# Reading the inverse row sums instead of every q and k block in the range check of an unshifted exp

## The chip, the cores and the metric

The kernel runs on one core of a Trainium2 chip. The metric is the device time of one execution in microseconds. A core has five engines that run side by side, each through its own queue: PE (TensorE, matrix products), VectorE (DVE in the profile), ScalarE (ACT), GpSimd (POOL) and SyncE (SP). Medians are quoted with the range of their runs.

## The reference

Two independent attention problems, A and B, whose outputs are put side by side. The shapes are 2048 tokens, width 1024, 32 heads of 32, and a causal window of 256 keys.

```python
def _A_ref(x, wqkv, wo):                       # _B_ref is the same
    B, S, D = x.shape
    H = 32; Dh = D // H; W = 256
    qkv = (x @ wqkv).reshape(B, S, 3, H, Dh)    # q, k, v, heads in front
    scores = einsum("bhqd,bhkd->bhqk", q, k) * (Dh ** -0.5)
    mask = (i - j >= 0) & (i - j < W)
    p = softmax(where(mask, scores, -1e9))
    return (p @ v, heads merged) @ wo
```

x and both weights are 0.05 times normal numbers in bf16.

## The kernel before

The quick path takes exp(score - SHIFT) with a constant SHIFT instead of the row's maximum. That is right only while the scores are moderate, so a check runs beside it, and if it fails, a slow path with a true softmax computes everything again. Before, the check ORs the bits of every q and k block into one tile `top`, and at the end compares the largest magnitude seen with 2.0.

The program is not written in the order of its execution. A planner in Python deals out matmul chains and, for each result in PSUM (one of two banks, `pp`), picks the engine that copies it to SBUF, with a crude clock of its own for each engine. VectorE's smaller work waits in a list `side`.

```python
class _Clock:
    def evacuate(self, engines):
        best = min(engines, key=lambda e: max(getattr(self, e), self.pe) + COST[e])
        end = max(getattr(self, best), self.pe + 150.0) + COST[best]
        setattr(self, best, end)
        ...
def evacuate(out, in_, engines=("act", "dve")):
    if clock.evacuate(engines) == "act":
        nc.scalar.copy(out=out, in_=in_)
    else:
        nc.vector.tensor_copy(out=out, in_=in_)
def add_or(dst):                       # after each evacuated q or k block: the end of the list
    def f():
        nc.vector.tensor_tensor(out=top[:], in0=top[:], in1=dst.bitcast(I32),
                                op=ALU.bitwise_or)
    side.append((COST["or"], f, False))
...                                    # in pv(), per pair of query blocks, after its matmuls into acc
    def f():
        nc.vector.reciprocal(out=rinv[:], in_=acc[:, 2 * P:3 * P])
    pieces.append((COST["rinv"], f, False))
    def f():
        for h in range(2):
            nc.vector.stream_shuffle(out=wide[:, h * P:(h + 1) * P], in_=rinv[:], ...)
        nc.vector.tensor_tensor(out=oTs[...], in0=acc[:, 0:256], in1=wide[:], op=ALU.mult)
    pieces.append((COST["mult"], f, True))
    n = max([i + 1 for i, x in enumerate(side) if x[2]], default=0)
    side[n:n] = pieces                 # ahead of waiting ORs
...                                    # in the main loop: an edge is two additions for a pair's row sums
    while edges_due and edges_due[0][0] <= now:
        edge(*edges_due.pop(0)[1:])
    ...
    if now >= sealed and len(certify) == 2:
        while side:
            run_side()
        certify.pop(0)(top)            # AND, maximum, comparison on VectorE
    elif now >= sealed + 2 and len(certify) == 1:
        certify.pop(0)(ps_proj)        # 1x1 matmul: sum of the verdicts, read by VectorE
```

## Time and profile before

The median was 609.52 us (609.34 to 609.76, 3 runs).

| engine | busy us | share | what it does |
|---|---|---|---|
| PE | 593.6 | 98% | projections, scores, attention, output |
| VectorE | 468.4 | 77% | additions, reciprocals, shuffles, multiplies, ORs, 66 evacuations |
| ScalarE | 441.1 | 73% | 180 exps, 189 evacuations of 512 columns |
| GpSimd | 326.3 | 54% | masks |

An engine at 98% leaves nothing for the others to shorten except its waits. The prediction below shows those lines.

### The profile page before, as it was taken

The page shows a single profiled execution, that of the slowest core. Times are in us where ns is not written, and L with a number is a line of the kernel's source. Part 1 is how long each engine was busy: PE and PEld are TensorE (multiplying, and loading weights), DVE is VectorE, ACT ScalarE, POOL GpSimd, SP SyncE. Part 2 cuts the span into 40 slices and gives each one's busy share as a digit, 9 for nine tenths or more (in the row PEclk, how much of TensorE's full clock was granted, in tenths as well). Part 3 has the DMA queues.
Part 4 walks back from the last instruction along what each step waited for, and adds up shares of the span by engine and source line. Part 5 has one row for each costly group of instructions (what it writes and reads, how often), then busy time and mean ns, then how long its engine had stood idle before and what let it go on. Part 6 is the DMA issues. An engine that isn't in the chain of part 4 may idle for free.

```text
span 607.6 us, 28768 instructions
## 1 busy us (share of the span) xinstructions
PE 593.6 (98%) x12786; PEld 344.3 (57%) x12838; DVE 468.4 (77%) x1199; ACT 441.1 (73%) x376; POOL 326.3 (54%) x630
## 2 busy tenths in 40 slices
PE   8999999999999999999999999999999999999996
PEld 6555466656655756564556756655455665545443
DVE  1677889898898898897888887898888887897200
ACT  3778887788888887877778877777776777785332
POOL 0565666665666666556555565555555655554000
PEclk9999999999999999999999999999999999999999
DMA  9833110111015501442111100112021040113222
GB/s 234 182 92 89 37 38 3 38 38 39 3 38 90 114 14 30 82 101 77 38 37 38 38 4 8 33 37 81 2 68 34 4 106 21 55 58 120 72 79 64
DMA packets 86802, 35.47 MB, mean 58 GB/s; under 512 B 65552, under 2 KB 86160, under 8 KB 86672
## 3 DMA queue, kind: packets, MB, share of 16 engines
q1 hardware_dynamic: 85632, 33.31, 22.2%
q8 instruction: 102, 1.67, 1.2%
q10 hardware_dynamic: 1040, 0.26, 0.2%
q14 instruction: 28, 0.23, 0.1%
HBM read 17.83 MB, written 8.39 MB: 43 GB/s over the span
## 4 chain that ended last, share of the span: by engine, by line
PE 96%; ACT 2%; issue 1%; DMA 1%; ACTq 0%
PE pp L176 44%; PE pp L172 28%; PE acc L513 13%; PE st L451 10%; ACT pt L459 1%; DMA oT<-in_A_x_dram 1%; PE acc L582 0%; PE pp L568 0%; ACT kT L190 0%; ACT vt L190 0%; PE st L582 0%; ACT osb L190 0%; PE pp L805 0%; ACTq L190 0%
## 5 line engine op out<-in xcount | busy, mean ns | idle before, releaser
L459 ACT ACTIVATE pt<-st 128x2048 bf16<-128x2048 f32 x180 | 338.0, 1878 | 91.6 <-PE st L451 73.5
L471 POOL TENSOR_SCALAR_AFFINE_SELECT pt<-pt 128x512 bf16<-128x512 bf16 x224 | 154.5, 690 | 145.7 <-ACT pt L459 143.1
L467 POOL TENSOR_SCALAR_AFFINE_SELECT pt<-pt 128x512 bf16<-128x512 bf16 x256 | 179.2, 701 | 85.8 <-ACT pt L459 85.8
L524 DVE RECIPROCAL rinv<-acc 128x128 f32<-128x128 f32 x128 | 122.0, 953 | 57.0 <-PE acc L513 56.4
L176 PE MATMUL pp<-xT,wqk 128*32 128x512 bf16 x2712 | 163.1, 379 | 0.0
L481 DVE TENSOR_TENSOR both<-pt 128x512 bf16<-128x512 bf16 x224 | 137.1, 651 | 0.0
L176 PEld LDWEIGHTS <-wqk 128*32 128x32 bf16 x2712 | 69.3, 97 | 54.2 <-issue 0.4
L172 PE MATMUL pp<-xT,wqk 128*128 128x512 bf16 (+1 forms) x323 | 76.7, 369 | 4.1 <-issue 2.4
L176 PE MATMUL pp<-wv,xT 128*32 128x256 bf16 x2436 | 75.9, 273 | 0.0
L451 PE MATMUL st<-qT,kT 32*128 32x384 bf16 (+2 forms) x1488 | 71.5, 269 | 0.1
L176 PEld LDWEIGHTS <-xT 128*32 128x32 bf16 x2436 | 63.8, 97 | 6.2
L529 DVE STREAM_SHUFFLE wide<-rinv 128x128 f32<-128x128 f32 x256 | 64.6, 298 | 0.0
L513 PE MATMUL acc<-pt,vt 128*32 128x128 bf16 (+1 forms) x2160 | 63.3, 239 | 0.0
L172 PE MATMUL pp<-wo_sb,oT 128*128 128x512 bf16 (+1 forms) x269 | 59.3, 373 | 1.3 <-issue 0.9
L451 PEld LDWEIGHTS <-kT 32*128 32x128 bf16 x1488 | 22.2, 92 | 64.5 <-issue 63.3
L190 ACT CAST osb<-pp 128x512 bf16<-128x512 f32 (+1 forms) x52 | 30.0, 577 | 39.1 <-PE pp L172 24.4
L531 DVE TENSOR_TENSOR oT<-acc,wide 128x256 bf16<-128x256 f32 x128 | 54.3, 425 | 4.4
L176 PE MATMUL pp<-wo_sb,oT 128*32 128x512 bf16 x952 | 55.6, 379 | 0.0
L172 PEld LDWEIGHTS <-wqk 128*128 128x128 bf16 x362 | 33.4, 98 | 37.0 <-issue 6.8
L172 PE MATMUL pp<-wv,xT 128*128 128x256 bf16 x415 | 50.9, 273 | 1.4 <-ACT kT L190 0.6
L513 PEld LDWEIGHTS <-vt 128*32 128x32 bf16 x2160 | 35.9, 96 | 26.4 <-issue 24.1
L172 PEld LDWEIGHTS <-xT 128*128 128x128 bf16 x415 | 38.9, 98 | 12.0 <-issue 6.1
(46 smaller groups left out, 386.5 us busy)
## 6 DMA issues: line engine op xcount, KB each, us to landing
out_dram<-osb SPq DMA_DIRECT2D x63, 128.0 KB, 1.8
wqk<-in_B_wqkv_dram SPq DMA_DIRECT2D x32, 128.0 KB, 2.5
wqk<-in_A_wqkv_dram SPq DMA_DIRECT2D x24, 128.0 KB, 2.7
wo_sb<-in_A_wo_dram SPq DMA_DIRECT2D x16, 128.0 KB, 2.2
wv<-in_B_wqkv_dram SPq DMA_DIRECT2D x16, 128.0 KB, 2.8
wo_sb<-in_B_wo_dram SPq DMA_DIRECT2D x16, 128.0 KB, 2.4
oT<-in_A_x_dram SPq DMA_DIRECT2D x4, 256.0 KB, 5.4
wv<-in_A_wqkv_dram SPq DMA_DIRECT2D x2, 512.0 KB, 5.9
```

Of the source, the lines that this page charges most:

```text
L172: nc.tensor.matmul(out[:, lo:hi], lhsT=lhsT, rhs=rhs, start=start, stop=stop, skip_group_check=True)
L176: nc.tensor.matmul(out[c:c + 32, lo:hi], lhsT=lhsT[:, c:c + 32], rhs=rhs, start=start, stop=stop, tile_position=(0, c), skip_group_check=True)
L190: nc.scalar.copy(out=out, in_=in_)
L451: nc.tensor.matmul(st[:, r, a:b, :], lhsT=kT[32 * r:32 * r + 32, j * P:(j + 1) * P], rhs=qT[32 * r:32 * r + 32, q * P:(q + b - a) * P], st ...
L459: nc.scalar.activation(out=pt[:, :, :n, :].rearrange("p r a q -> p r (a q)"), in_=st[:, :, :n, :].rearrange("p r a q -> p r (a q)"), func= ...
L467: nc.gpsimd.affine_select(out=blk, in_=blk, pattern=[[0, 4], [1, P]], compare_op=ALU.is_ge, fill=0.0, base=0, channel_multiplier=-1)
L471: nc.gpsimd.affine_select(out=blk, in_=blk, pattern=[[0, 4], [-1, P]], compare_op=ALU.is_gt, fill=0.0, base=0, channel_multiplier=1)
L481: nc.vector.tensor_tensor(out=both[:, :, h, :], in0=pts[s0][:, :, a0, :], in1=pts[s1][:, :, a1, :], op=ALU.add)
L513: nc.tensor.matmul(acc[32 * r:32 * r + 32, o:o + w_], lhsT=lhsT, rhs=src[:, r, :, :], start=(x == 0), stop=(x == len(moves) - 1), tile_pos ...
L524: nc.vector.reciprocal(out=rinv[:], in_=acc[:, 2 * P:3 * P])
L529: nc.vector.stream_shuffle(out=wide[:, h * P:(h + 1) * P], in_=rinv[:], mask=[16 * h] * 32)
L531: nc.vector.tensor_tensor(out=oTs[(pi, k)][:, t, (p % 2) * 256:(p % 2 + 1) * 256], in0=acc[:, 0:256], in1=wide[:], op=ALU.mult)
```

## The change

The intent is to relieve VectorE. A softmax row whose scores are moderate has a sum, and so an inverse, within a known power-of-two range, and the inverse is there anyway. One operation per two pairs XORs its bits with 2.0's and ORs them into `top`; bits 29 and 30 must stay clear. As the last inverse comes at the end, so does the verdict. SHIFT changes so that the inverses fall into the range.

```diff
+IN_RANGE = 0x40000000
+OUT_OF_RANGE = 0x60000000
+SHIFT = 33.0 * math.log(2.0) - math.log(1.9)
...
                     evacuate(dst, st_["pp"][:])
-                    add_or(dst)
...
-        rinv = normp.tile([P, P], F32, name="rinv")
+        turn = g * NP + p
...
+            if turn % 2 == 0:
+                inverses[0] = normp.tile([P, 2, P], F32, name="rinv")
+            nc.vector.reciprocal(out=inverses[0][:, turn % 2, :], in_=acc[:, 2 * P:3 * P])
...                                   # in the multiply's piece, behind the multiply
+            if turn % 2:
+                nc.vector.scalar_tensor_tensor(
+                    out=top[:], in0=inverses[0][:].rearrange("p h q -> p (h q)").bitcast(I32),
+                    scalar=IN_RANGE, in1=top[:], op0=ALU.bitwise_xor, op1=ALU.bitwise_or)
-        pieces.append((COST["mult"], f, True))
+        pieces.append((COST["mult"] + (COST["or"] if turn % 2 else 0.0), f, True))
...                                   # the verdict: out of the loop, behind the last multiply
     finish_norm()
+    certify[0](top)
+    emit(END + 10, 2 * NS_MM * CT)
+    certify[1](ps_proj)
     emit(END + 10, float("inf"))
```

More of the change, by code (lines that the diff above doesn't have):

```diff
@@ L20 @@
 KEYS_PER_QUERY = 3 * P
-CERT = 30.0
-SHIFT = 53.0 * math.log(2.0) - math.log(1.9)
-assert SHIFT >= CERT + math.log(KEYS_PER_QUERY)
+IN_RANGE = 0x40000000
+OUT_OF_RANGE = 0x60000000
+SHIFT = 33.0 * math.log(2.0) - math.log(1.9)
+assert math.log(KEYS_PER_QUERY) < SHIFT < 62.0 * math.log(2.0)
 MASK_NEG = -1.0e9
-QK_LIMIT = 2.0
-QK_LIMIT_BITS = 0x4000
 QB = 4
@@ L122, in _fast_path @@
     edges = {}
+    inverses = [None]
     top = once.tile([P, 256], I32, name="top")
@@ L180, in _fast_path @@
     whole = [True]
-    def add_or(dst):
-        def f():
-            nc.vector.tensor_tensor(out=top[:], in0=top[:], in1=dst.bitcast(I32),
-                                    op=ALU.bitwise_or)
-        side.append((COST["or"], f, False))
     def evacuate(out, in_, engines=("act", "dve")):
@@ L523, in f @@
         def f():
-            nc.vector.reciprocal(out=rinv[:], in_=acc[:, 2 * P:3 * P])
+            if turn % 2 == 0:
+                inverses[0] = normp.tile([P, 2, P], F32, name="rinv")
+            nc.vector.reciprocal(out=inverses[0][:, turn % 2, :], in_=acc[:, 2 * P:3 * P])
         pieces.append((COST["rinv"], f, False))
@@ L528, in f @@
             for h in range(2):
-                nc.vector.stream_shuffle(out=wide[:, h * P:(h + 1) * P], in_=rinv[:],
+                nc.vector.stream_shuffle(out=wide[:, h * P:(h + 1) * P], in_=inverses[0][:, turn % 2, :],
                                          mask=[16 * h] * 32)
@@ L603, in _fast_path @@
     emit(0, chains[0].size)
-    sealed = first_use(G - 1, NQ - 1, 0)
     for now in range(END):
@@ L616, in _fast_path @@
         emit(now, level(now) - fixed[now])
-        if now >= sealed and len(certify) == 2:
-            while side:
-                run_side()
-            certify.pop(0)(top)
-        elif now >= sealed + 2 and len(certify) == 1:
-            certify.pop(0)(ps_proj)
-    assert not certify
     while edges_due:
@@ L793 @@
     consts = {"ones": ones, "ident": ident}
-    assert DH * QK_LIMIT * QK_LIMIT * cfg.scale <= CERT
     def reduce_bits(top):
         seen = top[:]
-        nc.vector.tensor_single_scalar(out=seen, in_=seen, scalar=0x7FFF7FFF, op=ALU.bitwise_and)
-        nc.vector.tensor_reduce(out=pm[:], in_=seen.bitcast(I16), axis=AX.X, op=ALU.max)
-        nc.vector.tensor_scalar(out=okp[:], in0=pm[:], scalar1=float(QK_LIMIT_BITS), scalar2=None,
+        nc.vector.tensor_single_scalar(out=seen, in_=seen, scalar=OUT_OF_RANGE, op=ALU.bitwise_and)
+        nc.vector.tensor_reduce(out=pm[:], in_=seen, axis=AX.X, op=ALU.max)
+        nc.vector.tensor_scalar(out=okp[:], in0=pm[:], scalar1=0.5, scalar2=None,
                                 op0=ALU.is_lt)
```

## The prediction

> **What bounds the kernel now.** I read the page first, for the engine that has no slack. Columns: busy time, share of the span, instructions; then the busy share in 40 slices.
>
> ```profile
> PE 593.6 (98%) x12786; PEld 344.3 (57%) x12838; DVE 468.4 (77%) x1199; ACT 441.1 (73%) x376; POOL 326.3 (54%) x630
> ...
> PE   8999999999999999999999999999999999999996
> ...
> DVE  1677889898898898897888887898888887897200
> ```
>
> PE is at 9 tenths or more in every slice but the first and the last, DVE is not full in any long stretch. A busy PE is not yet a PE that never waits, so the second view is PE's waits between 10 and 565 us, that is without the start and the tail (columns: engine and line, what it waited for, us in total, times, longest).
>
> ```profile
> PE pp L172 <- issue: 3.5, 22, 0.2
> PE pp L172 <- ACT vt L190: 1.0, 2, 0.5
> PE pp L172 <- ACT kT L190: 0.6, 2, 0.4
> PE pp L172 <- DVE oT L531: 0.3, 2, 0.2
> ```
>
> 5.4 us in 555. The "issue" part belongs to PE's own stream, and the two DVE entries are 0.16 us each, as long as the usual issue gap, so I count them with it. What other engines really cost PE in the loop is four stalls of ScalarE, 0.39 + 0.49 + 0.49 + 0.19 = 1.56 us. Third, the chain that ended last, at one of the four, says how they arise:
>
> ```profile
> 71.84 0.36 PE st L451 x8
> 72.20 0.02 issue
> 72.22 1.88 ACT pt L459
> 74.10 0.49 ACT kT L190
> 74.58 0.04 issue
> 74.63 0.38 PE pp L172 x2
> ```
>
> A projection ended just after an exp had started, ScalarE could evacuate its PSUM bank only behind that exp, and the next projection but one needed the bank. VectorE is in none of the four. So VectorE, where the whole change lies, has 1.56 us of PE time within its reach at the very most, and only if it takes such an evacuation over. Fourth, the groups of instructions, for prices (count, busy us, mean ns, idle before them):
>
> ```profile
> L184 DVE TENSOR_TENSOR top<-top,kT 128x256 int32<-128x256 int32 x64 | 35.2, 549 | 0.9 <-ACT kT L190 0.5
> L184 DVE TENSOR_TENSOR top<-top,qT 128x256 int32<-128x256 int32 x64 | 32.4, 507 | 1.9 <-ACT qT L190 1.3
> L192 DVE CAST kT<-pp 128x512 bf16<-128x512 f32 x19 | 12.9, 678 | 7.8 <-PE pp L176 5.1 <-PE pp L172 2.7
> ```
>
> **What the Trainium skill says.** "TensorE: Matmul & The Clock Gate", section "Wait — 56ns, not 53.3ns?", gives a warm matmul a pitch of N / 2.4 GHz + about 2.5 ns, 215.7 ns at 512 columns. In the tail the evacuations of eight-matmul chains start 1.727 us apart, 215.9 ns per matmul: PE streams at its rate there, and a saving elsewhere cannot speed it up. "VectorE: DVE Perf Modes", section on the TRN2 errata, gives an fp32 tensor_tensor of N elements (N + 151) / 0.96 ns, 424 ns at 256; the ORs' medians are 417 ns (q) and 464 ns (k), so it holds for undisturbed ones. Their means of 507 and 549 fit "SBUF — State Buffer", section "Who interferes with whom": a DVE instruction with two SBUF inputs contends with a GpSimd one that reads SBUF, and the later one blocks. The trace has ORs from 407 up to 896 ns and GpSimd selects from 628 up to 924 ns. The new operation also has two SBUF inputs, so I price it as the old one. "DVE: scalar operands, raw-bit mode, write accounting and state across instructions", section 2, says that an immediate in bit-vector mode is a raw 32-bit pattern; the old check ends with such an AND and its run took the fast path, so I expect the new XOR and AND to be exact too.
>
> **The change part by part.**
> 1. Removed: 128 ORs over q and k blocks, 35.2 + 32.4 = 67.6 us of VectorE.
> 2. Added: one XOR-then-OR per two pairs, 128 / 2 = 64, over 128x256 words. At the ORs' mean, (549 + 507) / 2 = 528 ns, that is 33.8 us (estimate). It stands right behind the multiply that frees the accumulator, so it does not delay that release.
> 3. Moved by the planner: it counts VectorE as less loaded and gives it more evacuations. In the built order I count 79 PSUM evacuations of 512 columns on VectorE, before 66; 176 on ScalarE, before 189. At 674 ns (the mean of the 66) VectorE gets 13 x 0.674 = 8.8 us more, at 584 ns ScalarE gets 7.6 us less. Sum: VectorE 468.4 - 67.6 + 33.8 + 8.8 = 443 us (73%), ScalarE 441.1 - 7.6 = 433.5 us (71%). All of it lies beside PE's stream.
> 4. PE: its instruction order is identical in both, GpSimd's too, but for one instruction, the 1x1 matmul that adds up the verdict. So PE's work is the same to the instruction, and its time changes only by waits.
> 5. The waits in the loop. I went through the order for every reuse of a projection bank that ScalarE evacuates and compared when PE wants the bank with when the evacuation can end (exp 1.88 us, evacuation 0.59 us, matmuls at the pitch above). In the kernel before, the four tightest places are the four stalls of the trace, with 0.55 to 0.86 us too little; those that lack 0.35 us or less did not stall. The stall is thus about the lack less 0.35 us. In the changed order the four are gone, VectorE evacuates there, but five others lack 0.85, 0.75, 0.66, 0.55 and 0.45: 0.50 + 0.40 + 0.31 + 0.20 + 0.10 = 1.5 us. Net 0.0.
> 6. The verdict. Before, it is decided inside the loop:
>
> ```profile
> 556.99 0.16 PE L805 MATMUL pp<-okp,ones 128*1 128x1 f32 x1
> ...
> 557.01 0.16 PE L805 MATMUL pp<-okp,ones 128*1 128x1 f32 x1
> 557.04 0.49 PE L513 MATMUL acc<-pt,vt 128*32 128x128 bf16 x17
> ...
> 557.22 0.14 DVE L806 TENSOR_SCALAR unsafe_i<-pp 1x1 int32<-1x1 f32 x1 [1.15 <-PE pp L805]
> ...
> 557.57 3.64 PE L176 MATMUL pp<-wo_sb,oT 128*32 128x512 bf16 x64
> ```
>
> The next projection writes the same bank and waits until VectorE has read the sum, but 0.9 us of attention matmuls go in between, so it costs PE nothing. In the changed order the sum stands between two output projections of the tail, and the very next matmul waits for VectorE's read (the bank is the same, the order shows the wait). From 556.99 to 557.36 plus some 0.05 us of signalling: PE stands still for about 0.4 us. That lies on the path: +0.4 us.
> 7. Is the sum's own input late? The last multiply ends at 567.8; the XOR (0.9 at most), AND, reduction and comparison (0.61 + 0.69 + 0.15 in the old check) end by 570.2. PE gets to the sum after 32 matmuls from 565.71, at 572.6. No wait. After it come 16 whole and two half stores, near 29 us, so the branch at the end finds its verdict ready.
>
> Sum: 609.5 + 0.0 + 0.4 = 609.9 us.
>
> **The rivals.** (a) VectorE's relief speeds the kernel: 77% busy and 25 us less to do looks like a gain. For it: an engine that lags would free banks and accumulators late. Against it: no PE wait on VectorE beyond the issue gap. It can give back 1.56 us at most if all four stalls go and no new one comes: 608.4 with the tail's cost. (b) More VectorE evacuations stall PE instead: its queue is in order, and an evacuation behind a reciprocal (0.95 us), shuffles and the 0.65 us additions comes late. For it: 13 more of them, and the new operation keeps the reciprocal's successor waiting. Against it: 66 such evacuations caused no stall. Five stalls of 0.4 us would make 611.9. (c) The check fails and the slow path runs: many times the time. The scores here are close to 0 (x and w are 0.05 times normal numbers), so a row sum of 1 to 256 keys is about 1.9 x 2^-33 times that count, its inverse 2^24 to 2^32; bit 30 is set and bit 29 clear from 2 to 2^65. I give it under 1%. (d) The check at the end lengthens the finish, because the sum waits for VectorE or all engines for the verdict: part 7 leaves 2.4 us and 29 us of slack.
>
> **Range and chances.** Runs of the kernel before span 0.4 us. Part 5 is the uncertain one, from -1.5 to +1.5 us; new VectorE stalls lean upwards. Predicted 609.9, range 608.7 to 611.2. Two per cent is 12 us, more than all waits of PE in the loop together (5.4), so faster by that is all but excluded (0.01); slower needs the slow path or a failure of the order (0.02); the same 0.97.
>
> **What would show it.** VectorE near 443 us and ScalarE near 433 us busy; 64 new operations at 0.42 to 0.6 us; PE busy 593 to 594 us; in PE's waits four to six ScalarE evacuations of 1 to 2 us in total, at other times than before; one wait of about 0.4 us on VectorE's read of the verdict near 573 us. I am wrong if VectorE evacuations appear in PE's waits with over 1 us, if PE's busy time moves by more than 1 us, or if the ScalarE stalls vanish altogether.

## The result, and the profile after

The changed kernel took 611.24 us (611.07 to 611.60, 4 runs) beside 609.64 us of before: ratio 1.0027, interval 1.0010 to 1.0045. It is slower by 1.6 us, where +0.4 was predicted; 611.24 lies just outside the range that ended at 611.2.

The first line of the page after (busy us, share, instructions):

```profile
PE 599.8 (98%) x12838; PEld 345.0 (57%) x12838; DVE 437.3 (72%) x1148; ACT 434.8 (71%) x363; POOL 317.8 (52%) x630
```

VectorE lost 31 us and ScalarE 6, as intended. PE's busy time seems to have grown by 6 us, but it has 12838 matmul records here, as many as weight loads, and only 12786 before: the trace before lacks 52. The gaps that they leave had been listed there as 22 "issue" waits, 3.5 us in all. After, there are none. All thirteen traces agree: the eight with 12786 records list an "issue" wait, the five with 12838 list none. PE's waits after (what it waited for, us in total, times, longest; the first is the start):

```profile
PE pp L567 <- DVE ones L777: 1.3, 1, 1.3
PE pp L172 <- ACT qT L184: 0.8, 3, 0.4
PE acc L506 <- DVE oT L526: 0.7, 1, 0.7
PE pp L172 <- ACT vt L184: 0.5, 1, 0.5
PE pp L172 <- ACT kT L184: 0.4, 1, 0.4
PE pp L172 <- DVE unsafe_i L799: 0.2, 1, 0.2
```

There are five ScalarE stalls (0.8 + 0.5 + 0.4 = 1.7 us), the wait for the verdict, and one that the prediction did not have: PE waits 0.70 us for an accumulator that VectorE's multiply (oT) frees late.

Both traces hold the same weight loads in the same order, so subtracting their start times shows where the time is lost. Each number is a step of the difference "after minus before"; the offset of 0.15 us at the start is left out, since it varies between -0.3 and +0.9 us from profile to profile.

```
us        step    what PE's waits show there
75        -0.35   ScalarE stall of before gone
126       +0.57   new ScalarE stall (0.41 idle)
142       -0.65   stall of before gone
147       +0.78   late accumulator (0.70 idle)
158, 174  +0.25, +0.35   new ScalarE stalls (0.19 idle each)
225, 242  -0.50, -0.66   stalls of before gone
374, 385  +0.55, +0.63   new ScalarE stalls (0.39, 0.50 idle)
572       +0.49   verdict (0.24 idle)
rest      +0.38   (100: +0.17, 117: +0.09, 251: +0.16, 319: -0.17, 487: +0.13)
sum       +1.84
```

The sum agrees with the 1.6 us of the timed runs to their scatter. Gone are 2.16 us, new at ScalarE 2.35, VectorE's late accumulator 0.78, the verdict 0.49 (the weight loads of the verdict's own sum are left out when the traces are aligned; 0.3 of it is the wait for VectorE, the rest the small sum itself).

A stall costs up to 0.17 us more than its idle time. This is how the profile counts: the record of a 512-column matmul lasts 379 ns, but the next one starts after 216 ns, so idle time begins only 163 ns after the next matmul could have started. The starts say the same: 788 ns apart at 126 us, and 788 - 216 = 572 ns is the step there.

How the accumulator comes late is in the chain that ended last, which here leaves PE and runs along VectorE (start us, us, engine and tile):

```profile
140.29 0.95 DVE rinv L519
141.24 1.18 DVE both L474 x2
142.41 0.54 DVE vt L186
142.95 0.50 DVE wide L524 x2
...
143.81 0.69 DVE top L529
144.50 1.54 DVE both L474 x2
146.04 0.88 DVE rinv L519
...
147.97 0.74 PE acc L506 x36
```

The planner had given the v block at 142.4 us to VectorE. Its queue is in order. Two additions and this evacuation (1.18 and 0.54 us) stood between a reciprocal (done at 141.2) and that reciprocal's shuffles and multiply, so these ran at 142.95 to 143.9. VectorE was not idle before the evacuation, so it lost no time there by waiting for its matmul. Then the new operation (0.69 us) and two more additions stood in front of the next reciprocal, and the next multiply ended at 147.9 instead of 147.0. Before, shuffles and multiply followed the reciprocal at once and were done at 141.6, and the next reciprocal had 1.02 us to spare (VectorE's timeline of the kernel before, idle time in brackets):

```profile
139.66 0.95 DVE L524 RECIPROCAL rinv<-acc 128x128 f32<-128x128 f32 x1
140.65 0.29 DVE L529 STREAM_SHUFFLE wide<-rinv 128x128 f32<-128x128 f32 x1
...
141.19 0.42 DVE L531 TENSOR_TENSOR oT<-acc,wide 128x256 bf16<-128x256 f32 x1
141.53 0.41 DVE L184 TENSOR_TENSOR top<-top,kT 128x256 int32<-128x256 int32 x1
141.86 0.75 DVE L481 TENSOR_TENSOR both<-pt 128x512 bf16<-128x512 bf16 x2
142.53 0.42 DVE L184 TENSOR_TENSOR top<-top,qT 128x256 int32<-128x256 int32 x1
142.87 1.19 DVE L481 TENSOR_TENSOR both<-pt 128x512 bf16<-128x512 bf16 x2
145.07 0.96 DVE L524 RECIPROCAL rinv<-acc 128x128 f32<-128x128 f32 x1 [1.02 <-PE acc L513]
...
146.62 0.42 DVE L531 TENSOR_TENSOR oT<-acc,wide 128x256 bf16<-128x256 f32 x1
```

The verdict in the tail (timeline: start us, us, engine, line, operation, tiles, idle before it):

```profile
574.18 0.19 PE L798 MATMUL pp<-okp,ones 128*1 128x1 f32 x2
...
574.41 0.15 DVE L799 TENSOR_SCALAR unsafe_i<-pp 1x1 int32<-1x1 f32 x1 [3.86 <-PE pp L798]
574.61 5.55 PE L172 MATMUL pp<-wo_sb,oT 128*128 128x512 bf16 x25 [0.24 <-DVE unsafe_i L799]
```

PE goes on 0.43 us after it began the sum, as the prediction had it. VectorE had idled 3.86 us, so the sum did not wait for the check.

The groups of the new operation and of the additions after (count, busy us, mean ns, idle before):

```profile
L474 DVE TENSOR_TENSOR both<-pt 128x512 bf16<-128x512 bf16 x224 | 126.5, 605 | 0.8 <-PE acc L506 0.8
...
L529 DVE SCALAR_TENSOR_TENSOR top<-rinv,top 128x256 int32<-128x256 int32 x64 | 37.0, 578 | 0.0
```

### The profile page after: what moved, and what is told of

The parts are those of the page before. It is cut to its first block, busy times and chain, and to the rows that moved or that the text cites. A ratio compares the mean times of both kernels' runs of the same rounds, so it can differ in the third digit from the quotient of the medians.

```text
span 609.6 us, 28777 instructions
## 1 busy us (share of the span) xinstructions
PE 599.8 (98%) x12838; PEld 345.0 (57%) x12838; DVE 437.3 (72%) x1148; ACT 434.8 (71%) x363; POOL 317.8 (52%) x630
## 4 chain that ended last, share of the span: by engine, by line
PE 73%; DVE 3%; issue 1%; ACT 1%; DVEq 0%; ACTq 0%
PE pp L176 34%; PE pp L172 22%; PE acc L506 11%; PE st L444 7%; DVE both L474 1%; DVE rinv L519 1%; DVE wide L524 1%; ACT pt L452 0%; DVE top L529 0%; DVE oT L526 0%; DVE vt L186 0%; ACT qT L184 0%; ACT kT L184 0%; ACT vt L184 0%; ACT osb L184 0%
## 5 line engine op out<-in xcount | busy, mean ns | idle before, releaser
L464 POOL TENSOR_SCALAR_AFFINE_SELECT pt<-pt 128x512 bf16<-128x512 bf16 x224 | 149.4, 667 | 153.1 <-ACT pt L452 153.1
L460 POOL TENSOR_SCALAR_AFFINE_SELECT pt<-pt 128x512 bf16<-128x512 bf16 x256 | 175.6, 687 | 88.2 <-ACT pt L452 88.2
L474 DVE TENSOR_TENSOR both<-pt 128x512 bf16<-128x512 bf16 x224 | 126.5, 605 | 0.8 <-PE acc L506 0.8
L172 PE MATMUL pp<-xT,wqk 128*128 128x512 bf16 (+1 forms) x362 | 82.7, 370 | 0.6 <-ACT qT L184 0.6
L172 PE MATMUL pp<-wo_sb,oT 128*128 128x512 bf16 (+1 forms) x282 | 61.4, 373 | 0.2 <-DVE unsafe_i L799 0.2
```

The source lines that it names most:

```text
L172: nc.tensor.matmul(out[:, lo:hi], lhsT=lhsT, rhs=rhs, start=start, stop=stop, skip_group_check=True)
L460: nc.gpsimd.affine_select(out=blk, in_=blk, pattern=[[0, 4], [1, P]], compare_op=ALU.is_ge, fill=0.0, base=0, channel_multiplier=-1)
L464: nc.gpsimd.affine_select(out=blk, in_=blk, pattern=[[0, 4], [-1, P]], compare_op=ALU.is_gt, fill=0.0, base=0, channel_multiplier=1)
L474: nc.vector.tensor_tensor(out=both[:, :, h, :], in0=pts[s0][:, :, a0, :], in1=pts[s1][:, :, a1, :], op=ALU.add)
```

## The experiments

My first theory after the result: the evacuations moved by the planner cost 0.3 us net at ScalarE, the new operation makes the accumulator at 148 us late (0.8), the verdict costs 0.4. Its rivals: the operation as such costs everything; the moved evacuations cost everything. All eleven kernels gave right results and had five timed rounds; those of one heading ran on one chip with the same runs of before.

### First group (before: 609.50 us, 609.05 to 609.97)

**b_no_or**: before, ORs not issued. The check then guards nothing, on purpose.

```diff
-            nc.vector.tensor_tensor(out=top[:], in0=top[:], in1=dst.bitcast(I32),
-                                    op=ALU.bitwise_or)
+            pass
```

> The kernel before with its 128 ORs not issued; the planner and so every other instruction and its place are unchanged (the check then guards nothing, the result stays right). Theory 1 (PE bounds the kernel, VectorE's load lies beside it): VectorE's busy time falls by 67 us to about 400, the time stays within 0.4 us of 609.6, and the four ScalarE stalls (74, 143, 227, 244 us) stay. Rival (VectorE's load, or its contention with GpSimd for the SBUF port, slows the whole): 608.5 us or less.

Measured 610.03 us (608.87 to 610.09), ratio 1.0001 (0.9987 to 1.0015). VectorE's busy time fell from 468.4 to 400.8 us, the 67.6 us of the ORs to the tenth, and the four ScalarE stalls stayed where they were. The ORs cost nothing that these runs resolve (the interval leaves about 0.8 us either way; the aligned traces end 0.27 us ahead), so there was next to nothing to save by a cheaper check, with the rest in its place.

**a_no_op**: the changed kernel, new operation not issued; the planner still counts it.

```diff
-            if turn % 2:
-                nc.vector.scalar_tensor_tensor(
-                    out=top[:], in0=..., scalar=IN_RANGE, in1=top[:],
-                    op0=ALU.bitwise_xor, op1=ALU.bitwise_or)
```

> The changed kernel with its 64 XOR-OR operations not issued, everything else in its place. Theory 1 (the 1.6 us are: one late accumulator at 148 us for 0.8, five ScalarE stalls against four for 0.3, the verdict for 0.4): the operation at 143.8 us (0.69 us) delays the accumulator, so that the wait of 0.70 us at 148 us goes; the five ScalarE stalls and the verdict's wait stay; 610.4 us. Rival A (the operation itself costs the 1.6 us): 609.6. Rival B (only the moved evacuations cost, the operation nothing): 611.2, the wait at 148 us stays.

Measured 611.15 us (610.91 to 611.32), ratio 1.0026 (1.0012 to 1.0040). My first theory missed: without the operation the time is as good as the same. In the trace an accumulator is still late, at 150.75 us and by 0.44 instead of 0.70 us. By the aligned traces this kernel ends 1.31 us behind before, the changed one 1.83, so the operation may cost up to 0.5 us in this setting; the times do not resolve it.

**a_own_bank**: the changed kernel, the verdict's sum in an accumulator bank.

```diff
-        csum = pool.tile([P, 512], F32, name="pp")
+        csum = pool.tile([P, 512], F32, name="acc")
-    certify[1](ps_proj)
+    certify[1](ps_acc)
```

> The changed kernel with the verdict's sum in an accumulator bank that is free in the tail, so that the next projection need not wait for VectorE's read. Theory 1: the gap of about 0.4 us at 574 us goes, 610.8 us. Rival (the gap is the small matmul itself, or nothing is won since the end waits for the verdict): 611.1 to 611.3.

Measured 610.86 us (610.58 to 611.74), ratio 1.0023 (1.0009 to 1.0036). In the trace the wait is gone: PE goes on at 574.62 after a sum begun at 574.50. The verdict's step in the aligned traces falls from 0.49 to 0.2 us, so a part of it is the small sum itself and stays, as the rival had it; at the end this kernel is 1.45 us behind before, not 1.83. The times agree in sign, but their intervals overlap.

**b_after_plan**: before, each evacuation on the engine that the changed kernel uses. PLAN is the changed kernel's list of 257 choices. (Forced onto its own list, each kernel gave its own program again, instruction by instruction.)

```diff
-        best = min(engines, key=lambda e: max(getattr(self, e), self.pe) + COST[e])
+        best = {"a": "act", "d": "dve"}[PLAN[self.n]]
+        self.n += 1
```

> The kernel before, ORs and early verdict as they were, but each of its 257 evacuations on the engine that the changed kernel uses (43 differ). Theory 1: the five ScalarE stalls of the changed kernel (126, 159, 176, 375, 385 us) appear, the four of before go, +0.3 us; the accumulator at 148 us is late too if the evacuations in front of it suffice, which gives up to +0.8 more: 609.9 to 610.8 us. Rival (the placement costs nothing, only the new operation and the verdict do): 609.6 us.

Measured 611.47 us (611.22 to 612.05), ratio 1.0036 (1.0022 to 1.0049): above the expected range, and as slow as the changed kernel, with the old ORs and the early verdict. PE's waits of this run, without the start:

```profile
PE pp L180 <- DVE vt L200: 1.0, 2, 0.7
PE pp L180 <- ACT qT L198: 0.6, 2, 0.4
PE pp L180 <- ACT vt L198: 0.5, 1, 0.5
PE pp L180 <- ACT kT L198: 0.4, 1, 0.4
PE pp L180 <- DVE kT L200: 0.3, 1, 0.3
```

Four of the changed kernel's five ScalarE stalls are listed here (the fifth is too short for the list, but its step of 0.35 us is in the aligned traces), and where before had ScalarE stalls (143, 227, 245 us) PE now waits for VectorE's evacuations. Moving 43 evacuations, with nothing else changed in the mathematics, makes the slowdown by itself.

### Second group (before: 609.79 us, 609.10 to 610.27)

My second theory: placement costs the loop its time, the operation nothing.

**a_before_plan**: the changed kernel with before's list of 257 choices in PLAN, otherwise the edit of b_after_plan.

> The changed kernel with every one of its 257 evacuations on the engine that the kernel before uses: the new operation and the late verdict alone, without the moved evacuations. Theory 2 (the moved evacuations cost the loop its time, the operation nothing; the verdict 0.3 us): the four ScalarE stalls of before are back (74, 143, 227, 244 us), the five of the changed kernel and the late accumulator at 148 us are gone, the verdict's wait stays: 609.9 us. Rival (the new operation in its place costs as well): 610.6 us or more.

Measured 611.06 us (610.49 to 611.57), ratio 1.0023 (1.0009 to 1.0036). The second theory fell too. The four ScalarE stalls were back and the five and the late accumulator gone, as expected, but two steps of 0.24 and 0.34 us were new at 374 and 384 us. There PE waited for a v block on VectorE (0.20 us idle at 384.69). VectorE in front of it (timeline):

```profile
382.38 0.55 DVE L537 SCALAR_TENSOR_TENSOR top<-rinv,top 128x256 int32<-128x256 int32 x1
382.85 1.18 DVE L482 TENSOR_TENSOR both<-pt 128x512 bf16<-128x512 bf16 x2
383.96 0.68 DVE L194 CAST vt<-pp 128x512 bf16<-128x512 f32 x1
```

The new operation stands ahead of the evacuation. In the kernel before, the ORs came behind the same evacuation, because they were the end of the list:

```profile
381.66 1.32 DVE L481 TENSOR_TENSOR both<-pt 128x512 bf16<-128x512 bf16 x2
382.91 0.68 DVE L192 CAST vt<-pp 128x512 bf16<-128x512 f32 x1
383.51 0.41 DVE L184 TENSOR_TENSOR top<-top,qT 128x256 int32<-128x256 int32 x1
```

**a_side_first**: the changed kernel with its own choices forced, but before VectorE is given an evacuation, all pending work is issued.

```diff
         else:
+            while side:
+                run_side()
             nc.vector.tensor_copy(out=out, in_=in_)
```

> The changed kernel, same engine for each evacuation, but before VectorE is given an evacuation all pending reciprocal and multiply work is issued to it. Theory 2 says that the accumulator at 148 us is late because VectorE's in-order queue held that work behind an evacuation (142.3 us) that still waited for its matmul: the wait of 0.7 us goes, the five ScalarE stalls and the verdict stay, 610.5 us. Rival (the work in front makes the evacuations late in turn): new VectorE waits in PE's list, 611 us or more.

Measured 622.16 us (622.01 to 622.36), ratio 1.0205 (1.0191 to 1.0219): the rival, and far more of it than expected. Two of its wait lines:

```profile
PE pp L180 <- DVE vt L196: 2.1, 3, 1.0
PE pp L180 <- DVE kT L196: 1.9, 6, 0.6
```

The late accumulator did vanish, but now evacuations wait behind reciprocals, some of which themselves wait for matmuls. Work behind an evacuation is late in one order, evacuations are late in the other, and the second is much worse.

**a_hybrid**: the changed kernel, before's choices except the four stalled evacuations, which go to VectorE, and the verdict in its own bank (edits as above, PLAN differing from before's in four letters).

> The changed kernel with the placement of before except its four stalled evacuations, which go to VectorE (28th, 56th, 90th and 97th of 257), and the verdict in a free accumulator bank. Theory 2: no ScalarE stall is left, a late accumulator near 148 us may remain (0 to 0.8): 607.4 to 608.2 us. Rival (VectorE stalls take their place, as with the ORs in b_after_plan, where PE waited 0.3 to 0.7 us for VectorE at 143, 227 and 245 us): 608.8 us or more.

Measured 608.79 us (608.59 to 609.33), ratio 0.9987 (0.9974 to 1.0001). This was between the two expectations, at the edge of the rival's. No ScalarE stall is left. The late accumulator (0.70 us idle at 146.9) and the steps at 374 and 384 us (0.24 and 0.34) remain.

**b_hybrid**: before, ORs and early verdict, with the same PLAN.

> The kernel before with its ORs and early verdict, and the same four evacuations moved to VectorE. Theory 2: the stall at 74 us goes, those at 143, 227 and 245 us turn into waits for VectorE, which the ORs keep busy there, as in b_after_plan: 609.0 us. Rival (the new operation is of no use even with the better placement): as a_hybrid, within 0.4 us.

Measured 609.55 us (608.51 to 610.37), ratio 0.9991 (0.9977 to 1.0005). The stall at 74 us went, and at 144, 227 and 245 us PE waited 0.33, 0.20 and 0.68 us for VectorE, as expected. The intervals of the two hybrids overlap, so their times alone do not rank them.

### Third group (before: 609.78 us, 609.11 to 610.12)

My third theory: the operation costs by its place in VectorE's in-order queue, not by its length.

**a_late_op**: as a_before_plan, the operation moved from behind the multiply to just before the next pair's reciprocal (and, in the planner's costs, with it; this also shifts other VectorE work).

```diff
+            if turn % 2 == 0:
+                check()               # the XOR-OR over the last two pairs
                 inverses[0] = normp.tile([P, 2, P], F32, name="rinv")
...
-            if turn % 2:
-                nc.vector.scalar_tensor_tensor(...)
...
+    check()
     certify[0](top)
```

> As a_before_plan, but each new operation is issued just before the next pair's reciprocal instead of right behind the multiply, so that additions and evacuations that follow the multiply are no longer behind it. Theory 3 (the operation costs by its place: in a_before_plan it stands in front of two evacuations, at 374 and 384 us, which then come 0.24 and 0.34 us late; the ORs stood behind them): those two steps go, 610.4 us, 0.6 less than a_before_plan; the four ScalarE stalls and the verdict stay. Rival (the 374 and 384 us steps come from something else in the queue): as a_before_plan, 611.0.

Measured 610.09 us (609.86 to 610.45), ratio 1.0007 (0.9994 to 1.0021), 1.0 us less than a_before_plan (on another chip; each beside its own runs of before, 0.3 against 1.3 us). Both steps are gone, and on VectorE the operation now comes behind the evacuation:

```profile
382.21 0.68 DVE L194 CAST vt<-pp 128x512 bf16<-128x512 f32 x1
...
385.21 0.41 DVE L543 SCALAR_TENSOR_TENSOR top<-rinv,top 128x256 int32<-128x256 int32 x1
```

But the operation is not all that moved: in a_before_plan the pair's shuffles and multiply ran at 381.5 to 382.5, ahead of this evacuation, and here they run at 382.8 to 383.8, behind it. So the run does not show the operation's place alone. In the aligned traces what remains is the verdict's step (0.43 us in all).

**a_hybrid_late**: a_hybrid with this edit.

> a_hybrid with the operation just before the next reciprocal. Theory 3: the steps at 374 and 384 us go (0.6), and the accumulator at 147 us, which was 0.7 us late with the operation in front of its reciprocal, is no better, since the operation now stands directly ahead of a reciprocal there too, or it moves to the next one: 607.9 to 608.3 us. Rival (place does not matter): 608.8.

Measured 607.89 us (607.36 to 608.51), ratio 0.9972 (0.9958 to 0.9985). Faster than both kernels, a little better than expected: the accumulator is no longer late either, because in this order the shuffles and the multiply precede the additions at 139 to 141 us. PE's waits:

```profile
PE pp L180 <- issue: 3.8, 24, 0.2
PE pp L578 <- DVE ones L789: 1.3, 1, 1.3
PE pp L180 <- DVE vt L194: 0.2, 1, 0.2
```

Beyond the start, one wait of 0.19 us is left. (The "issue" entry is back with the missing records: this trace has 12786 matmuls.) It is still within 2% of before; PE's list of waits had no more to give. No run gives the ORs this order, so how much of the gain is due to the cheaper check is not shown.

**a_hybrid_late_edge**: a_hybrid_late, and a multiply whose reciprocal is done goes ahead of the additions.

```diff
         while edges_due and edges_due[0][0] <= now:
+            if side and side[0][2]:
+                run_side()
             edge(*edges_due.pop(0)[1:])
```

> a_hybrid_late, and a multiply whose reciprocal is done is issued before the additions for the next pair instead of behind them. Theory 2 (the accumulator at 147 us is late because its multiply stood behind two additions and an evacuation that waited for its matmul): that wait goes, no PE wait on another engine over 0.3 us is left, 607.3 us. Rival (the additions then come late and PE waits for them, or the accumulator stays late): 608 us or more.

Measured 610.75 us (610.22 to 611.19), ratio 1.0016 (1.0002 to 1.0030). A miss: the accumulator at 147 us was not late, but it had not been in a_hybrid_late either. The reordering put a wait of 1.13 us at 47.8 us, an attention matmul behind VectorE's late evacuation of a v block, and others of 0.46 and 0.52 us at 245 and 309 us. Applied everywhere, the order does harm here.

## Why the prediction was wrong

**Part 1, the ORs lie beside PE: right.** b_no_or takes away 67.6 us of VectorE and no time that the runs resolve.

**Part 2, the new operation: price near, place wrong.** 37.0 us measured against 33.8 estimated. What failed here is the sentence that it "stands right behind the multiply that frees the accumulator, so it does not delay that release". It is true of that release and overlooks what follows in the queue. The ORs were the end of VectorE's list; the new operation is part of the multiply's piece, ahead of additions, evacuations and the next reciprocal. a_before_plan, with the order of before but for the operation, shows 0.6 us of trace steps where the operation stands ahead of evacuations. That its place counts and not its length is argued, since a_late_op moved the multiply as well. In the changed kernel the operation is worth at most some 0.5 us by the aligned traces (a_no_op), so this is not the main miss; that is in part 5.

**Part 3, the moved evacuations: right in number.** VectorE 437 us against 443 predicted: the miss is mainly the additions, which fell by 10.6 us, from 137.1 to 126.5 (651 to 605 ns each), a term that the sum did not have, against 3.2 us more for the new operation. ScalarE 434.8 against 433.5.

**Part 4: right.** Apart from the verdict PE ran the same instructions. The claim that PE's busy time would be 593 to 594 us failed, for the missing records.

**Part 5, the waits in the loop: this is the step that failed, "Net 0.0".** At ScalarE the mechanism was right. The four stalls went and five came, of 0.50, 0.39, 0.41, 0.19 and 0.19 us where 0.50, 0.40, 0.31, 0.20 and 0.10 had been worked out. But idle time was taken for the cost: in PE's starts a stall is mostly some 0.16 us longer, and with five for four that makes 2.35 - 2.16 = +0.19 us. The larger part was left out: I compared only ScalarE's evacuations with their banks, not VectorE's work with its accumulators: +0.78 us.

**Rival (b), VectorE comes late instead: this is what happened, the other way round.** I argued against it that 66 evacuations on VectorE had caused no stall. That was evidence for those 66 in their places. Also, I had feared evacuations behind reciprocals; in the changed kernel it was a reciprocal's successors behind two additions and an evacuation. (Some of my expectations say that this evacuation waited for its matmul; VectorE was not idle before it, so this was wrong.) b_after_plan shows the placement alone making 611.47 us.

**Part 6, the verdict: right, a little small.** 0.43 us from the sum to PE's next matmul, a step of 0.49 us in the aligned traces, of which 0.3 us is gone in a_own_bank. **Part 7: right**, VectorE was done at 570.6, PE came at 574.2.

Two slips changed nothing: the rivals' 608.4 us should be 608.3, and GpSimd's selects go up to 1212 ns, not 924, on the other of their two lines.

So the sum was +0.4 and should have been 0.19 + 0.78 + 0.49, with small steps of 0.38 us that I have not traced one by one. The contributions do not simply add: without the operation (a_no_op) or without the placement (a_before_plan) most of the loss is still there, because each puts other VectorE work in the way. What is shown is that with both changed, and the verdict in its own bank (a_hybrid_late), the loss turns into a gain of 0.28%.

## What to carry to other kernels

When the bounding engine hardly waits, price a change on another engine by what stands behind each moved instruction in its in-order queue, not by its busy time; and when a planner sees the lower load, look at every decision that it changes, for they can cost more than the change itself. Evidence that "none of these caused a wait" holds for the old places only. Check the count of records before reading a gap as a wait.

## What the Trainium skill lacked or had wrong

- "VectorE: DVE Perf Modes" has no price for scalar_tensor_tensor. With two SBUF inputs of 128x256 words it took 412 ns at least, 482 in the median, 578 in the mean; the page's tensor_tensor formula (424 ns for 256 elements, an estimate from it, since the page measured 512 and 2048) is near the least.
- "SBUF — State Buffer", section "Who interferes with whom", agrees with the runs but gives no size for a mix like this one: in the changed kernel the 150 additions that overlap GpSimd work took 702 ns in the mean, the other 74 took 408. The mean of all 224 does not follow the number of other two-input operations: 651 ns before with 128 of them, 605 with 64, but 607 without any (b_no_or) and 557 with 64 in a_side_first. The check's AND over 128x256 words took 606 ns when a GpSimd selection had begun before it, 282 ns when it had begun just before the selection (b_no_or), and 294 ns with GpSimd idle.
- "Perfetto Trace Analysis" does not say that matmul records can be missing from a trace and then look like short waits: 12786 of 12838 records, with 22 gaps of up to 0.2 us, 3.5 us in all, in the kernel before; none of either in the changed one.
- No page that I read puts a size on order in VectorE's in-order queue: issuing its pending work ahead of its evacuations cost about 1.8% of the changed kernel (a_side_first, ratio 1.0205 to before, where the changed kernel has 1.0027).
- "TensorE: Matmul & The Clock Gate" gives pitch and latency of matmuls, but not what follows for reading a trace: their difference, here 379 - 216 = 163 ns at 512 columns, is missing from the idle time shown (steps of 0.65 and 0.35 us for 0.49 and 0.19 us of idle time).
